# Causal mask carried in the unused contraction rows of q and k, in a fused attention and gated-convolution kernel

## The chip, the cores and the metric

The kernel runs on one core of a Trainium2 chip. The core has five engines with queues of their own: TensorE (PE, with its weight loads shown as PEld), VectorE (DVE), ScalarE (ACT), GpSimd (POOL) and SyncE (SP), which issues most of the DMAs. Each engine takes its instructions strictly in the order in which they were written; semaphores join the queues. The metric is the device time of one execution in microseconds.

## The reference

q, k and v are (8, 8, 576, 64) in float32, for 8 batches and 8 heads. f (8, 8, 576) holds forget gates. An attention with decay and a causal mask feeds a feed-forward layer whose gate is a convolution over the sequence:

```
scores = q @ k.T / sqrt(64) + cum[query] - cum[key]     # cum = cumsum(log(clip(f, 1e-4, 1)))
scores[key > query] = -1e9
attn = softmax(scores);  x = (attn @ v), heads side by side, (8, 576, 512)
h = relu(x @ w_in)                                        # (8, 576, 1024)
gate = sigmoid(conv of h over the sequence, 3 taps per channel)
out = (h * gate) @ w_out                                  # (8, 576, 512)
```

## The kernel before

**Half batches.** The attention is worked in 16 half batches (`hb`) of four heads. A sequence of 576 is cut into four key blocks of 128 and a tail of 64. Scores are computed with keys on the partitions. For each pair of heads there is one task for the four diagonal blocks (`sd`), two for the blocks below the diagonal (`so`), and for each half batch one for the tail (`st`). ScalarE takes the exponential of each (`ed`, `eo`, `et`), PE multiplies by v with a column of ones beside it (`pv`), VectorE divides (`n` the reciprocal, `m` the product), and the result is turned for the next layer by PE (`t`) and copied out (`tx`). The feed-forward tasks are, for each batch and each of 8 channel blocks: `f` on PE (w_in), `r` on ACT (relu), `c` and `d` on DVE (convolution), `a` on ACT, `g` on DVE (gate); then `o` on PE (w_out), `e` and `s` (copy out and store).

**Even and odd rows.** A float32 value is used as bf16 through its upper half. The turned q and k have 128 rows for 64 elements: the odd rows are the upper halves, the even rows are the lower halves, which are of no use. The contraction on PE runs over all 128 rows, so the even rows are free to carry something else. In the kernel before, three of them carry the decay and the rest are zero. For half batches 0 and 1, q and k are loaded plain and turned by PE (`tp`), then copied out by `turned_qk` (`cl`). The others are turned by a DMA (`load_qk`, task `q{hb}.{side}`, L180). In half batches 2 to 7 a clamp on VectorE (`cl{hb}.{side}`, L186) multiplies each row by 0 or 1 and adds the row's constant; then `rw{hb}` writes the decay rows by two small DMAs (L202, L203) from the DRAM tile `image`. In half batches 8 to 15 `fi{hb}` overwrites the even rows by DMAs from `blank` (zeros) and `image`. Half batch 0 adds the decay by two more matmuls per block (`by_matmul`).

**The causal mask** is applied in two ways. In half batches 0 to 7 (`MASK_PE`) PE first writes -1e30 above the diagonal into the bank with a matmul of `ident` and `mask` (L320) and adds the scores to it. In half batches 8 to 15 ScalarE writes the exponentials in float32 to `pd` or `p3`, and POOL copies them to `pp` or `pt` with an affine select that puts zeros above the diagonal (L356, L335; tasks `md`, `mt`).

**Order.** Nothing is scheduled while the program runs. The string `ORDER` is one list of task names; `Plan.play` goes through it and writes each task's instructions to its engines, and gives out buffers from rooms of fixed size (4 PSUM tiles `ps`, 6 of `pp`, 5 of `ht`, 4 of `u`). Where a task has several possible engines, `@` behind its name chooses one. The dependencies that the instructions wait for are those of the data and of the reused buffers.

## Time and profile before

| what | value |
|---|---|
| time, median of 3 runs | 247.56 us (247.29 to 249.18) |
| span of the profiled execution | 244.1 us |
| time of the profiled execution beside its span | not recorded; the median of the runs is 3.5 us above the span |
| granted TensorE clock | 0.999 |
| PE / DVE / ACT / POOL busy | 226.9 / 205.1 / 206.9 / 52.9 us |
| clamps, L186 | 12, 874 ns each, from 23.5 to 81.2 us |
| mask matmuls, L320 | 40, of which 32 are 128x512 |
| affine selects, L356 and L335 | 16 of 1244 ns, 8 of about 0.6 us |

A row of groups reads: line, engine, operation, out<-in with shapes, count | busy us, mean ns of one | idle time of the engine just before them and what ended it. A row of a timeline reads: start, duration, engine, line, operation, and in brackets the idle time before it with what ended it. A row of windows gives the stretch, its length, the busy time of each engine, the granted clock, the DMA share and the rate. In the chain, `issue` is time in which the engine waited for nothing that the profile shows; SPq, DVEq and so on are the engines' own issue work.

### The profile page before, as it was taken

How to read it: one execution, taken by the hardware profiler on the slowest of the kernel's cores; microseconds unless marked ns; L12 is line 12 of the kernel's file. 1: busy time of each engine (PE TensorE's matmuls, PEld its weight loads, DVE VectorE, ACT ScalarE, POOL GpSimd, SP SyncE). 2: the span in 40 equal slices, each digit the busy share in tenths (PEclk: the TensorE clock that was granted, in tenths of full speed). 3: DMA queues.
4: the chain of work that ended last, by engine and by line, in shares of the span. 5: the costliest groups of instructions: out<-in, count | busy, mean ns of one | idle time of the engine just before them, and what ended most of it. 6: DMA issues, size and time to landing. Idle time of an engine off the chain costs nothing.

```text
span 244.1 us, 6385 instructions
## 1 busy us (share of the span) xinstructions
PE 226.9 (93%) x2627; PEld 145.0 (59%) x2627; DVE 205.1 (84%) x323; ACT 206.9 (85%) x278; POOL 52.9 (22%) x77
## 2 busy tenths in 40 slices
...
GB/s 192 328 159 243 304 204 192 202 253 279 204 188 205 228 158 240 229 314 186 198 256 246 187 209 257 273 134 222 194 260 188 236 140 3 168 157 62 142 86 216
DMA packets 120176, 49.68 MB, mean 204 GB/s; under 512 B 109759, under 2 KB 110271, under 8 KB 120147
## 3 DMA queue, kind: packets, MB, share of 16 engines
...
q10 hardware_dynamic: 166, 0.31, 0.4%
...
HBM read 21.11 MB, written 10.17 MB: 128 GB/s over the span
## 4 chain that ended last, share of the span: by engine, by line
PE 78%; DVE 7%; DMA 6%; ACT 4%; issue 1%; ACTq 1%; SPq 1%; DVEq 0%
PE ps L474 24%; PE ps L429 20%; PE ps L312 15%; PE ps L389 7%; DMA qk<-in_q_dram 3%; PE ps L320 3%; PE ps L394 3%; PE ps L166 2%; PE ps L414 2%; DVE u L446 2%; ACT pp L370 2%; DMA pd<-in_moe_conv_w_dram 2%; DVE u L448 2%; DVE qk L186 1%; DMA qk<-image 1%
## 5 line engine op out<-in xcount | busy, mean ns | idle before, releaser
L429 PE MATMUL ps<-xt,w_in_f 128*128 128x512 f16 (+1 forms) x512 | 69.9, 286 | 0.0
L370 ACT ACTIVATE pp<-ps 128x1024 f16<-128x1024 f32 x64 | 64.7, 1032 | 4.2 <-PE ps L312 2.7
L474 PE MATMUL ps<-w_out_f,hg 128*128 128x512 f16 x288 | 66.8, 379 | 0.0
L312 PE MATMUL ps<-qk 128*128 128x128 bf16 (+2 forms) x576 | 63.4, 240 | 1.6 <-ACT pp L353 0.8
L446 DVE SCALAR_TENSOR_TENSOR u<-ht,cwt 128x576 f32<-128x576 f16 x64 | 52.7, 837 | 3.6 <-ACT ht L440 3.4
L451 ACT ACTIVATE hg<-u,cw 128x576 f16<-128x576 f32 x64 | 48.7, 782 | 5.9 <-DVE u L448 5.8
L448 DVE SCALAR_TENSOR_TENSOR u<-ht,cwt,u 128x576 f32<-128x576 f16 x64 | 53.2, 846 | 0.5
L429 PEld LDWEIGHTS <-w_in_f 128*128 128x128 f16 x512 | 34.3, 98 | 28.5
L312 PEld LDWEIGHTS <-qk 128*128 128x128 bf16 x576 | 39.2, 98 | 19.8 <-issue 3.3
L440 ACT ACTIVATE ht<-ps 128x576 f16<-128x576 f32 x64 | 41.0, 663 | 6.0 <-DVE hg L458 2.7
L474 PEld LDWEIGHTS <-hg 128*128 128x128 f16 x288 | 26.9, 98 | 28.8
L458 DVE SCALAR_TENSOR_TENSOR hg<-hg,ht 128x576 f16<-128x576 f16 x51 | 38.7, 771 | 0.6 <-ACT hg L451 0.5
L356 POOL TENSOR_SCALAR_AFFINE_SELECT pp<-pd 128x1024 f16<-128x1024 f32 x16 | 19.7, 1244 | 53.6 <-ACT pd L353 53.6
L389 PE MATMUL ps<-va,pp 128*128 128x65 f16 x640 | 24.8, 193 | 1.1 <-DVE va L217 1.0
L389 PEld LDWEIGHTS <-pp 128*128 128x128 f16 x640 | 22.6, 97 | 3.7 <-DVE va L217 1.3
L405 DVE TENSOR_TENSOR xm<-ps,rc 128x896 f16<-128x896 f32 (+1 forms) x32 | 23.9, 751 | 0.5
L353 ACT ACTIVATE pp<-ps 128x1024 f16<-128x1024 f32 x16 | 16.6, 1039 | 4.7 <-PE ps L312 3.9
L353 ACT ACTIVATE pd<-ps 128x1024 f32<-128x1024 f32 x16 | 16.2, 1023 | 1.2 <-PE ps L312 1.0
L217 POOL CAST va<-vf 128x1024 f16<-128x1024 f32 x8 | 10.0, 1252 | 32.1 <-DMA vf<-in_v_dram 27.8
L320 PE MATMUL ps<-mask,ident 128*128 128x512 bf16 (+1 forms) x40 | 14.3, 359 | 1.5 <-ACT pp L370 0.8
L403 DVE RECIPROCAL rc<-ps 128x14 f32<-128x14 f32 (+1 forms) x32 | 6.7, 208 | 8.6 <-PE ps L394 5.5
L479 ACT COPY ob<-ps 128x1024 f32<-128x1024 f32 (+1 forms) x14 | 12.9, 919 | 0.3 <-issue 0.2
...
## 6 DMA issues: line engine op xcount, KB each, us to landing
...
```

The source lines that it names most:

```text
L312: nc.tensor.matmul(o, tk[:, h * S + k0:h * S + k0 + 128], tq[:, h * S + q0:h * S + q0 + n], start=first, stop=last and not by_matmul(hb, h))
L353: nc.scalar.activation(o, ps_of(f"sd{i}").rearrange("p (s c) -> p s c", s=2), AF.Exp, scale=SCALE)
L370: nc.scalar.activation(pair(i)[:, s, 512:1536], ps_of(f"so{i}.{s}"), AF.Exp, scale=SCALE)
L389: nc.tensor.matmul(ps[:, c:c + D + 1], block(hb, h, m, n), va[:, h, m, 0:D + 1], start=(m == 0), stop=(m == n))
L405: nc.vector.tensor_tensor(xm[:, CUT * D * u:CUT * D * u + nj * k * D].rearrange("p (j x d) -> p j x d", x=k, d=D), got[:, :, :, 0:D], r.un ...
L429: nc.tensor.matmul(ps[:, t0:t1], w_in_f16[:, cc, 128 * ff:128 * (ff + 1)], xt[:, cc // 2, x:x + t1 - t0], start=(cc == 0), stop=(cc == NCC ...
L440: nc.scalar.activation(ht_of(b, ff)[:, 2:2 + S], ps_of(f"f{b}.{ff}")[:, 0:S], AF.Relu, scale=1.0 if (b, ff) in LATE else 0.5)
L446: nc.vector.scalar_tensor_tensor(u, ht[:, 1:1 + S], cwt[:, ff, 0:1], ht[:, 2:2 + S], op0=ALU.mult, op1=ALU.add)
L448: nc.vector.scalar_tensor_tensor(u, ht[:, 3:3 + S], cwt[:, ff, 1:2], u, op0=ALU.mult, op1=ALU.add)
L451: nc.scalar.activation(hg_of(b, ff), u_t[slot[f"c{b}.{ff}", "u"]], AF.Sigmoid if (b, ff) in LATE else AF.Tanh, scale=cw[:, ff, 1:2])
L458: nc.vector.scalar_tensor_tensor(hv, hv, 1.0, ht_of(b, ff)[:, 2:2 + S], op0=ALU.add, op1=ALU.mult)
L474: nc.tensor.matmul(ps[:, 512 * (c % 2):512 * (c % 2 + 1)], w, w_out_f16[:, ff, :], start=(ff == 0), stop=(ff == NFF - 1))
```

## The change

The mask moves into the contraction. 55 of the 60 free even rows get a pattern, the same for every head: each row stands for a group of 6 positions of a 128-block (22 groups for blocks 0 and 1, 22 for 2 and 3, 11 for the tail). In q's row the values are powers of two that fall by 2^21 from one position of the group to the next; in k's row they are negative powers of two that rise by 2^21 per position and stay at the top behind the group. The product is -2^11 or below where the key lies after the query, and tiny elsewhere, in the off-diagonal blocks too. So `masked` with its matmuls (L320) is gone, and so are the affine selects and the tiles `pd` and `p3`; the exponentials of all half batches are written straight to `pp` and `pt`. The tail's scores use 64 partitions, not 128.

The pattern gets into the even rows in three ways:
- Half batches 0 and 1: PE turns the odd halves alone, to partitions 0 to 63. The pattern is computed densely on VectorE for partitions 64 to 127 of one head (`dense`), and copied to the other heads and to half batch 1 (`px0` on VectorE, `px1` on POOL).
- Half batches 2 to 7: the clamp becomes `blend`, a SCALAR_TENSOR_TENSOR that multiplies each row by 0 or 1 and adds the pattern tile `edge`, read again for each of the four heads. `edge` is written by `spread` (task `pi`) on POOL.
- Half batches 8 to 15: the fill reads from `shape`, a DRAM copy of the even rows of `edge`, in place of `blank`; two DMAs per half batch as before.

Four rows carry the decay now (two for q, two for k), so `rw` writes 2 rows by each of its two DMAs, and `image` is written by 4 DMAs, not 3. The identities and selectors are built by POOL, not VectorE, and the memsets are gathered in `pads` (task `pd`). In `ORDER`, `px0.0 px0.1` stand ahead of `dcs`, `pd` ahead of `va0.0`, `px1.0 px1.1 pi` behind `va0.1`; all `md`, `mt` are taken out, each `fi` is a `rw` in the same place, and all else keeps its place. All twelve blends are given to VectorE. The core of the diff:

```diff
+    BLEND = (2, 3, 4, 5, 6, 7,)
...
-    NCL = 8
-    MASK_PE = (0, 1, 2, 3, 4, 5, 6, 7,)
-    NPD, NP3 = 2, 2
...
-            nc.tensor.transpose(o[:, 128 * j:128 * (j + 1)], i[:, 128 * j:128 * (j + 1)], ident_b)
+            nc.tensor.transpose(o[0:64, 128 * j:128 * (j + 1)], i[:, 128 * j + 1:128 * (j + 1):2], ident_b)
...
-    def clamp(hb, h0, nh, side):
-        t = (stq_t, stk_t)[side][hb % RING].bitcast(U16)[:, h0 * S:(h0 + nh) * S]
-        nc.vector.tensor_scalar(t, t, lim[:, 2 * side:2 * side + 1], lim[:, 2 * side + 1:2 * side + 2],
-                                op0=ALU.mult, op1=ALU.add)
...
+    def blend(hb, side, e):
+        t = (stq_t, stk_t)[side][hb % RING].bitcast(U16)[:, 0:HS].rearrange("p (h s) -> p h s", h=HH)
+        pattern = edge[:, side].bitcast(U16).unsqueeze(1).broadcast_to((128, HH, S))
+        if e == "DVE":
+            nc.vector.scalar_tensor_tensor(t, t, lit[:, 2:3], pattern, op0=ALU.mult, op1=ALU.add)
+        else:
+            nc.gpsimd.tensor_scalar(t, t, lit[:, 2:3], None, op0=ALU.mult)
+            nc.gpsimd.tensor_tensor(t, t, pattern, op=ALU.add)
...
+    def edge_rows(t, side, e):
+        copy = {"ACT": nc.scalar.copy, "POOL": nc.gpsimd.tensor_copy, "DVE": nc.vector.tensor_copy}[e]
+        h = 1 if t == 0 else 0
+        o = qk_t[t][64:128, HS * side + h * S:HS * (side + 1)].rearrange("p (h s) -> p h s", s=S)
+        copy(o, qk_t[0][64:128, HS * side:HS * side + S].unsqueeze(1).broadcast_to((64, HH - h, S)))
...
     def fill(hb):
-        nc.sync.dma_start(even_rows(hb, 4, 60, 0, 2 * HS).rearrange("p (h s) -> p h s", s=2 * S),
-                          blank.unsqueeze(1).broadcast_to((60, HH, 2 * S)))
-        nc.sync.dma_start(even_rows(hb, 0, 4, 0, 2 * HS).rearrange("j (a x) -> j a x", a=2),
+        t = qk_t[hb % RING]
+        nc.sync.dma_start(rows(t, 8, 2, 60, 0, 2 * HS).rearrange("p (a h s) -> p a h s", a=2, s=2 * S),
+                          shape.rearrange("p a h s -> p a (h s)").unsqueeze(2).broadcast_to((60, 2, 2, 2 * S)))
+        nc.sync.dma_start(rows(t, 0, 2, 4, 0, 2 * HS).rearrange("j (a x) -> j a x", a=2),
...
-        nc.sync.dma_start(even_rows(hb, 1, 2, HS + h0 * S, 2 * HS), image[1:3, 1, c, :].rearrange("j h s -> j (h s)"))
+        c, t = slice(hb * HH, (hb + 1) * HH), qk_t[hb % RING]
+        for side in range(2):
+            r = 2 * side
+            nc.sync.dma_start(rows(t, 64 + r if hb < NPL else 2 * r, 1 if hb < NPL else 2, 2, HS * side, HS * (side + 1)),
+                              image[r:r + 2, side, c, :].rearrange("j h s -> j (h s)"))
...
+    turns = xm_t[0].bitcast(FP32), xm_t[1].bitcast(FP32), u_t[2], u_t[3], xt_t[0].rearrange("p a x -> p (a x)").bitcast(FP32)[:, 0:S]
+    base = turns[3]
+    dense = [qk_t[0][64:128, HS * side:HS * side + S].bitcast(U16) for side in range(2)]
+    SPAN, WHOLE, BOTH = GROUP + (FAR + 0.003) / STEP, float(-128 * STEP), float(128 * (FIRST - STEP + 2 * 127) + 32768)
...
+    def count(p0, per):
+        i = turns[0][p0:128].bitcast(I32)
+        nc.gpsimd.iota(i[:, 0:512], pattern=[[22 * GROUP, 2], [0, 2], [1, 128]], base=4 * GROUP, channel_multiplier=-per)
+        nc.gpsimd.iota(i[:, 512:S], pattern=[[1, SL]], base=48 * GROUP, channel_multiplier=-per)
+        return i
...
+    i = count(64, GROUP)
+    nc.gpsimd.memset(base, float(128 * (127 + TOP)))
+    nc.gpsimd.memset(base[:, 0:512].rearrange("p (a j s) -> p a j s", a=2, j=2)[:, :, 1], float(128 * (127 + LOW)))
...
-    nc.vector.tensor_scalar(mask, hfx, lit[:, 0:1], -1e30, op0=ALU.is_lt, op1=ALU.mult)
...
+    at, w, x = (turns[j][64:128] for j in range(3))
+    nc.vector.tensor_scalar(w, i, SPAN, None, op0=ALU.min)
+    nc.vector.scalar_tensor_tensor(x, w, WHOLE, base[64:128], op0=ALU.mult, op1=ALU.add)
+    nc.vector.scalar_tensor_tensor(at, w, 0.0, x, op0=ALU.is_ge, op1=ALU.mult)
+    nc.vector.scalar_tensor_tensor(dense[0], w, GROUP - 0.5, at, op0=ALU.is_le, op1=ALU.mult)
+    nc.vector.tensor_scalar(x, x, -1.0, BOTH, op0=ALU.mult, op1=ALU.add)
+    nc.vector.scalar_tensor_tensor(dense[1], w, 1.0, x, op0=ALU.is_ge, op1=ALU.mult)
+    for side, n, value in ((0, 4, 1.0), (0, 2, 0.0), (1, 4, 0.0), (1, 2, -1.0)):
+        nc.vector.memset(dense[side][0:n].bitcast(BF16), value)
...
+    nc.gpsimd.tensor_scalar(ident_b, hfx, lit[:, 0:1], None, op0=ALU.is_equal)
...
+    nc.gpsimd.tensor_scalar(ident, hfx, lit[:, 0:1], None, op0=ALU.is_equal)
...
+    def spread():
+        p = lit[:, 0:1]
+        nc.gpsimd.tensor_scalar(lit[:, 3:4], p, 7.5, None, op0=ALU.is_ge)
+        nc.gpsimd.tensor_scalar(lit[:, 4:5], lit[:, 2:3], 0.0, lit[:, 3:4], op0=ALU.is_equal, op1=ALU.mult)
...
+        at, w, x, y = (turns[j] for j in (0, 1, 2, 4))
+        i = count(0, GROUP // 2)
+        nc.gpsimd.tensor_scalar(w, i, SPAN, None, op0=ALU.min)
+        nc.gpsimd.tensor_scalar(x, w, WHOLE, None, op0=ALU.mult)
+        nc.gpsimd.tensor_tensor(x, x, base, op=ALU.add)
+        for side in range(2):
+            nc.gpsimd.tensor_scalar(at, w, float(side), None, op0=ALU.is_ge)
+            if side == 0:
+                nc.gpsimd.tensor_scalar(y, w, GROUP - 0.5, None, op0=ALU.is_le)
+                nc.gpsimd.tensor_tensor(at, at, y, op=ALU.mult)
+            else:
+                nc.gpsimd.tensor_scalar(x, x, -1.0, BOTH, op0=ALU.mult, op1=ALU.add)
+            nc.gpsimd.tensor_tensor(at, at, x, op=ALU.mult)
+            nc.gpsimd.tensor_scalar(edge[:, side].bitcast(U16), at, lit[:, 4:5], lit[:, 6 + side:7 + side], op0=ALU.mult, op1=ALU.add)
...
+    def pads():
+        for t in range(NVA):
+            nc.gpsimd.memset(va_t[t][:, :, :, D:VW], 1.0)
+            nc.gpsimd.memset(va_t[t][64:128, :, NKB - 1, 0:D], 0.0)
...
+        for t in range(NPT):
+            nc.gpsimd.memset(pt_t[t][64:128], 0.0)
...
-        nc.sync.dma_start(blank, zero[0:60])
...
+        even = bass.AP(tensor=edge.tensor, offset=int(edge.offset) + 8 * 2 * S, ap=[[2 * 2 * S, 60], [S, 2], [1, S]])
+        for h in range(2):
+            nc.sync.dma_start(shape[:, :, h], even)
...
+    def scores(o, hb, h, k0, q0, n, m=128):
...
-    def masked(o, n, j):
-        nc.tensor.matmul(o, ident, mask[:, 0:j].unsqueeze(1).broadcast_to((128, n, j)), start=True, stop=False)
...
     def tail_scores(hb):
-        on = hb in MASK_PE
-        if on:
-            masked(ps_of(f"st{hb}")[:, 0:HH * SL], HH, SL)
...
-            if on:
-                masked(ps[:, 512 * s:512 * (s + 1)], 4, 128)
...
-    def diag_mask(i):
-        nc.gpsimd.affine_select(pair(i)[:, :, 0:512].rearrange("p s (m j) -> p s m j", j=128),
-                                pd_t[slot[f"ed{i}", "pd"]].rearrange("p s (m j) -> p s m j", j=128),
-                                pattern=[[0, 2], [0, 4], [1, 128]], base=0, channel_multiplier=-1,
-                                compare_op=ALU.is_ge, fill=0.0)
...
+    add("ki", "SP", ["dck"], decay_image)
+    add("zc", "SP", ["pi", "pd"], constants)
...
+    add("pi", "POOL", [], spread)
+    add("pd", "POOL", [], pads)
+    for t in range(NPL):
+        for side in range(2):
+            add(f"px{t}.{side}", "POOL/DVE/ACT", [], lambda e, t=t, side=side: edge_rows(t, side, e))
...
-                add(f"rw{hb}", "SP", [f"cl{hb}.{p}.{side}" for p, side in parts] + ["ki"], lambda hb=hb: rows_of(hb))
-                ready = [[f"rw{hb}"]] * 2
+                add(f"rw{hb}", "SP", ["ki"] + px, lambda hb=hb: rows_of(hb))
+                ready = [[f"rw{hb}"] + [f"cl{hb}.{p}.{side}" for side in range(2)] for p in range(2)]
...
-            if hb < NCL:
-                for side in range(2):
-                    add(f"cl{hb}.{side}", "DVE", [f"q{hb}.{side}"], lambda hb=hb, side=side: clamp(hb, 0, 4, side))
-                add(f"rw{hb}", "SP", [f"cl{hb}.{side}" for side in range(2)] + ["ki"], lambda hb=hb: rows_of(hb))
-                ready = [[f"rw{hb}"]] * 2
+                add(f"q{hb}.{side}", "SP", old, lambda hb=hb, side=side: load_qk(hb, side))
+                if hb in BLEND:
+                    add(f"cl{hb}.{side}", "POOL/DVE", [f"q{hb}.{side}", "pi"], lambda e, hb=hb, side=side: blend(hb, side, e))
+            if hb in BLEND:
+                add(f"rw{hb}", "SP", ["ki"] + [f"cl{hb}.{side}" for side in range(2)], lambda hb=hb: rows_of(hb))
             else:
-                add(f"fi{hb}", "SP", [f"q{hb}.0", f"q{hb}.1", "zc", "ki"], lambda hb=hb: fill(hb))
-                ready = [[f"fi{hb}"]] * 2
+                add(f"rw{hb}", "SP", ["ki", "zc"] + [f"q{hb}.{side}" for side in range(2)], lambda hb=hb: fill(hb))
+            ready = [[f"rw{hb}"]] * 2
...
-            if hb not in MASK_PE:
-                add(f"md{i}", "POOL", [f"ed{i}"], lambda i=i: diag_mask(i), give=[("pd", f"ed{i}")])
+            add(f"ed{i}", "ACT", [f"sd{i}"], lambda i=i: diag_exp(i), give=[("ps", f"sd{i}")])
```

Three places show what the change does to the queues. First POOL, behind the start-up memsets. Before, the second cast of half batch 0's v (L219) is followed by a cast of w_in:

```order
L263 MEMSET va_94 64x4x64
L217 CAST va_91<-vf_89 128x4x4x64
L219 CAST va_91<-vf_89 64x4x64
L518 CAST w_in_f_69<-ob_125 128x2x512
L217 CAST va_92<-vf_89 128x4x4x64
L518 CAST w_in_f_69<-ob_126 128x2x512
```

Now (L221, L223 are those casts) the copies `px1` and then all of `spread` stand between; its last rows and the cast of w_in (L537) are the second piece:

```order
L221 CAST va_90<-vf_88 128x4x4x64
L223 CAST va_90<-vf_88 64x4x64
L189 COPY qk_85<-qk_84 64x2304 x2
L272 TENSOR_SCALAR lit<-lit 128x1
L273 TENSOR_SCALAR lit<-lit 128x1
```

```order
L292 TENSOR_TENSOR xm_104<-xm_104,u_118 128x576
L293 TENSOR_SCALAR edge<-xm_104,lit 128x576
L286 TENSOR_SCALAR xm_104<-xm_105 128x576
L291 TENSOR_SCALAR u_118<-u_118 128x576
L292 TENSOR_TENSOR xm_104<-xm_104,u_118 128x576
L293 TENSOR_SCALAR edge<-xm_104,lit 128x576
L537 CAST w_in_f_69<-ob_121 128x2x512
```

Between the two pieces stand the rest of the eight small operations, an iota and six operations on 128x576.

Second, VectorE at half batch 2, whose q and k lie in one tile (`qk_87` before, `qk_86` now). Before, the clamps wait for a DMA alone, and the norms of half batch 0 (L403, L405) follow:

```order
L174 TENSOR_SCALAR qk_86<-ps_131,lim 128x1152 [waits PE_49,Activation_49]
L186 TENSOR_SCALAR qk_87<-qk_87,lim 128x2304 [waits DMAHW2_49]
L186 TENSOR_SCALAR qk_87<-qk_87,lim 128x2304 [waits DMAHW6_49]
L403 RECIPROCAL rc_110<-ps_130 128x14 [waits PE_49,Activation_49]
L405 TENSOR_TENSOR xm_108<-ps_130,rc_110 128x896 [waits DVE_49]
```

Now each blend (L180) waits for POOL too, with the same norms (L422, L424) behind it:

```order
L168 COPY qk_85<-ps_127 64x1152 [waits PE_49,Activation_49]
L180 SCALAR_TENSOR_TENSOR qk_86<-qk_86,lit,edge 128x2304 [waits DMAHW3_49,Pool_49]
L180 SCALAR_TENSOR_TENSOR qk_86<-qk_86,lit,edge 128x2304 [waits DMAHW6_49,Pool_49]
L422 RECIPROCAL rc_106<-ps_126 128x14 [waits PE_49,Activation_49]
L424 TENSOR_TENSOR xm_104<-ps_126,rc_106 128x896 [waits DVE_49]
```

The place in the queue is the same; the operation and the wait are new.

Third, SP behind the loads of w_in. Before, the decay rows of half batch 2 (task `rw2`, to `qk_87`) stand ahead of the turned loads of half batches 3 and 4:

```order
L510 DMA ob_128<-in_moe_w_in_dram 128x2x512
L202 DMA qk_87<-image 1x2304
L203 DMA qk_87<-image 2x2304
L180 DMA_TRANSPOSE qk_88<-in_q_dram 128x2304
L180 DMA_TRANSPOSE qk_88<-in_k_dram 128x2304
L180 DMA_TRANSPOSE qk_85<-in_k_dram 128x2304
```

Now (L206 and L172, half batch 2 in `qk_86`) they stand there as well, and wait for the blends:

```order
L529 DMA ob_124<-in_moe_w_in_dram 128x2x512
L206 DMA qk_86<-image 2x2304 x2
L172 DMA_TRANSPOSE qk_87<-in_q_dram 128x2304
L172 DMA_TRANSPOSE qk_87<-in_k_dram 128x2304
L172 DMA_TRANSPOSE qk_84<-in_k_dram 128x2304
```

Nothing is reordered here; the rows behind `rw2` follow it as before.

164 lines of the change are left out of this document (60 added, 104 removed).

## The prediction

> **What bounds the kernel now.** I read the page first: the busy times, then the chain that ended last, by line.
>
> ```profile
> span 244.1 us, 6385 instructions
> ...
> PE 226.9 (93%) x2627; PEld 145.0 (59%) x2627; DVE 205.1 (84%) x323; ACT 206.9 (85%) x278; POOL 52.9 (22%) x77
> ...
> by line: PE ps L474 24.2%; PE ps L429 20.3%; PE ps L312 14.6%; PE ps L389 6.8%; DMA qk<-in_q_dram 3.0%; PE ps L320 2.7%; PE ps L394 2.5%; PE ps L166 2.4%; PE ps L414 2.2%; DVE u L446 2.1%; ACT pp L370 2.1%; DMA pd<-in_moe_conv_w_dram 2.0%;
> ```
>
> PE's lines carry most of the chain (the masks, L320, 2.7% of it), but 93, 84 and 85% are averages over stages, so the next view is the busy time by stage (the columns stand in its first row; times from the span's start).
>
> ```profile
> core 0: us, PE busy (x) PEld busy (x) DVE busy (x) ACT busy (x) POOL busy (x), PEclk, DMA share, GB/s
> 25.20:36.50 11.30, 10.12 (x173) 7.83 (x173) 4.46 (x9) 8.34 (x10) 5.14 (x5) 1.00 1.19 253
> 36.50:60.10 23.60, 20.27 (x278) 13.56 (x275) 23.26 (x35) 21.76 (x31) 4.39 (x4) 1.00 1.08 231
> 60.10:89.10 29.00, 29.00 (x338) 18.55 (x337) 27.24 (x42) 27.25 (x38) 5.42 (x5) 1.00 1.07 208
> 89.10:230.00 140.90, 140.79 (x1582) 86.00 (x1580) 131.57 (x197) 128.86 (x180) 31.24 (x31) 1.00 0.90 196
> ```
>
> Four stages with three limits. From 25 to 36 VectorE works 4.5 us out of 11. From 36.5 to 60 VectorE has 0.3 us to spare in 23.6 and PE has 3.3. From 60 to 89 PE has no gap, and VectorE only 1.8 us. After 89 PE is full for 141 us with VectorE 9 us under it. The chain in order of time says the same:
>
> ```profile
> 36.53 0.76 DVE xt L417
> 37.29 1.45 DVE qk L186 x2
> ...
> 57.77 1.01 DVE xm L405
> 58.82 0.83 PE ps L414 x9
> ...
> 222.65 3.92 PE ps L429 x32
> ```
>
> Between 36.5 and 58.8 the end hangs on VectorE and the loads behind its clamps, and the clamp itself (L186) is on the chain. From 58.8 on it hangs on PE, bar a few pieces. The change takes work off PE and puts it on VectorE, in just the stages where VectorE is full or nearly so.
>
> **What a blend costs.** Twelve clamps (half batches 2 to 7, q and k) turn from a TENSOR_SCALAR on one tensor into a SCALAR_TENSOR_TENSOR on two. Groups by line:
>
> ```profile
> L186 DVE TENSOR_SCALAR qk<-qk,lim 128x2304 uint16<-128x2304 uint16 x12 | 10.3, 874 | 2.3 <-DMA qk<-in_q_dram 2.3
> L458 DVE SCALAR_TENSOR_TENSOR hg<-hg,ht 128x576 f16<-128x576 f16 x51 | 38.7, 771 | 0.6 <-ACT hg L451 0.5
> L456 DVE TENSOR_TENSOR hg<-hg,ht 128x576 f16<-128x576 f16 x13 | 5.5, 451 | 1.0 <-ACT hg L451 1.0
> L405 DVE TENSOR_TENSOR xm<-ps,rc 128x256 f16<-128x256 f32 x16 | 6.6, 415 | 0.2
> L405 DVE TENSOR_TENSOR xm<-ps,rc 128x896 f16<-128x896 f32 x16 | 17.4, 1087 | 0.3
> ```
>
> The two forms of L405 give a slope of (1087 - 415) / 640 = 1.05 ns per element for an operation with two inputs at full width. Over 2304 elements that is 415 + 2048 x 1.05 = 2.57 us. The nearest row by operation is L458, all 16 bits wide and still 771 ns for 576 elements, on that same slope; so I take 2.55 us, **1.68 us more than a clamp**. The lower end is L456, a TENSOR_TENSOR on the same 16-bit tensors in 451 ns: 451 + 1728 x 0.525 = 1.36 us, 0.48 more. The upper end is four times L458, 3.08 us, 2.2 more.
>
> The Trainium skill, "VectorE: DVE Perf Modes", section "What auto-detection actually checks", says that two elements go through per cycle when every tensor is 16 bits wide with step 1. By that rule the blend would take the lower end; L458 meets its condition and does not show it, L456 does. What it would give is the second rival below.
>
> **Step A, the pattern comes late.** The blends of half batch 2 need the pattern that `spread` writes on POOL. On POOL it stands behind the casts va0 and two copies `px1` of 64x2304 each. POOL's rows:
>
> ```profile
> 16.53 1.04 POOL L217 CAST va<-vf 128x1024 f16<-128x1024 f32 x1 [10.07 <-DMA vf<-in_v_dram]
> 17.51 0.39 POOL L219 CAST va<-vf 64x256 f16<-64x256 f32 x1
> 25.70 1.04 POOL L518 CAST w_in_f<-ob 128x1024 f16<-128x1024 f32 x1 [7.80 <-DMA ob<-in_moe_w_in_dram]
> ...
> L356 POOL TENSOR_SCALAR_AFFINE_SELECT pp<-pd 128x1024 f16<-128x1024 f32 x16 | 19.7, 1244 | 53.6 <-ACT pd L353 53.6
> L335 POOL TENSOR_SCALAR_AFFINE_SELECT pt<-p 128x256 f16<-128x256 f32 x4 | 2.3, 584 | 4.1 <-ACT p L332 4.1
> L255 POOL MEMSET zero<- 64x1152 bf16 x1 | 1.0, 1049 | 0.0
> L262 POOL MEMSET va<- 128x40 f16 x4 | 0.5, 133 | 0.2
> L228 POOL IOTA hix<- 128x128 int32 x1 | 0.2, 234 | 0.0
> ```
>
> The casts wait for the load of v, so POOL is at 17.9 us there whatever the new memsets ahead cost (it idled 10 us). Then: two copies at the cast's rate (1.04 us for 1024), 2.3 us each, to 22.5. Eight operations of 128x1 at 0.133, 1.1 us. An iota of 576, at most 4.5 x 0.234 = 1.0. Twelve operations on 128x576, of which four have two inputs. For these the page has no row; between L335 and L356 the cost at 576 elements is 584 + 320 x 0.86 = 0.86 us, and I take that for all: 10.3 us. POOL ends `spread` at **35.0 us**, with q's half of the pattern ready four operations earlier, at 31.6. The lower end (the cast's 0.58 us per operation, the memset's rate for the copies, half the iota) is 30.7. The upper end (two-input operations twice as long, copies at L356's rate) is 39.4.
>
> The Trainium skill, "GPSIMD Engine Reference", section 3.1, gives 4497 ns for a two-input operation on 2048 elements; as an estimate that is 1.27 us for 576, and `spread` would end at 36.6 instead. No run so far shows such an operation.
>
> VectorE and PE around that time, with the load that follows a clamp:
>
> ```profile
> 23.50 1.67 DVE L186 TENSOR_SCALAR qk<-qk,lim 128x2304 uint16<-128x2304 uint16 x2 [2.25 <-DMA qk<-in_q_dram]
> ...
> 25.37 0.58 SPq L203 DMA_DIRECT2D qk<-image  x1
> ...
> 22.71 3.01 DMA qk<-image
> ...
> 31.16 0.39 PE L320 MATMUL ps<-mask,ident 128*128 128x512 bf16 x1
> ...
> 34.94 0.39 PE L320 MATMUL ps<-mask,ident 128*128 128x512 bf16 x1
> 35.16 0.39 PE L312 MATMUL ps<-qk 128*128 128x128 bf16 x4
> ```
>
> Before, the two clamps ended at 25.17, `rw2` was issued at 25.37 and, at the 3.01 us of its neighbour, landed at 28.4; PE came to `sd5`, the first scores of half batch 2, at 31.16. Now the first blend runs from 31.6 to 34.2, the second from 35.0 to 37.5. `rw2` lands near 41, and `sd5` follows its mask-free start there: before, its first score came 0.22 us behind the mask, at 31.38. PE is **9.6 us late**; the 2.8 us that `rw2` used to be early are spent. Everything is queued behind this. On VectorE the norms `n0.0` to `m1.1` stand behind the blends, on SP the loads of q and k for half batches 3 and 4 stand behind `rw2`, and on PE all that follows stands behind `sd5`. Three more masks are gone between there and 36.5, at 0.22 us each (the step from 34.94 to 35.16), so **+9.0 us** at 36.5.
>
> What else is added at the start is covered by this wait. VectorE gets six operations on 64x576, at 0.76 us each by the row below, and two copies `px0` that at the clamp's rate take under 0.9 each:
>
> ```profile
> 9.83 0.76 DVE L274 SCALAR_TENSOR_TENSOR kc<-u,kc 64x576 bf16<-64x576 f32 x1
> ```
>
> That is some 6 us, against the selectors and the mask that it built before and now leaves to POOL; `dck` and the first scores come perhaps 1.5 us later. `px1` ends at 22.5, and the load that waits for it, `rw1`, went at 22.71 anyway. All that is over before 31 us and would cost up to 1.5 us only if the wait at the blends were gone.
>
> **Steps B and C, ten blends.** The six of half batches 3 to 5 run from the pair on the chain at 37.29 to 59.23, the four of 6 and 7 from 75.36 on, the last two at 80.40:
>
> ```profile
> 59.23 0.87 DVE L186 TENSOR_SCALAR qk<-qk,lim 128x2304 uint16<-128x2304 uint16 x1
> ...
> 75.36 0.87 DVE L186 TENSOR_SCALAR qk<-qk,lim 128x2304 uint16<-128x2304 uint16 x1
> ...
> 80.40 1.66 DVE L186 TENSOR_SCALAR qk<-qk,lim 128x2304 uint16<-128x2304 uint16 x2
> ```
>
> B: from 36.5 to 60 VectorE has 0.3 us to spare: 6 x 1.68 = 10.1, **+10 us**. PE's masks here hide nothing, since PE already waits.
>
> C: 4 x 1.68 = 6.7 us against 1.8 us of slack from 60 to 89: **+4.9 us**. PE meets VectorE again here:
>
> ```profile
> 88.35 0.76 DVE L417 COPY xt<-ps 128x1152 f16<-128x1152 f16 x1 [0.18 <-PE ps L414]
> ...
> 89.56 1.14 PE L429 MATMUL ps<-xt,w_in_f 128*128 128x512 f16 x8
> ```
>
> The matmuls of batch 2 start 0.45 us behind the copy that feeds them, so PE takes the delay over nearly whole.
>
> **Step D, after 89.** PE is full and stays so. Of the masks, those left there, by the same windows for L320 alone:
>
> ```profile
> 60.10:89.10 29.00, 4.13 (x12) 1.17 (x12) 1.00 1.07 208
> 89.10:230.00 140.90, 2.06 (x6) 0.49 (x5) 1.00 0.90 196
> ```
>
> Six at 0.22 or less: **-1.0 us**. The others stand in stages where VectorE, not PE, sets the time, and are worth nothing beyond what A counted. The POOL selects of half batches 8 to 15 go away, 19.7 us and some, but POOL is 22% busy and PE never idles for them; the fills move the same bytes from `shape` as from `blank`.
>
> **Sum:** 9.0 + 10.1 + 4.9 - 1.0 = +23.0 us on the profiled span of 244.1, so about 267. The profiled execution has no time of its own beside the span; the median of the runs is 247.56, 3.5 above it. I carry the 3.5 over: 247.56 + 23.0 = 270.6, and say **271**.
>
> **The rivals.**
> 1. *The pattern is slower or quicker than 35.0.* Slower: at 39.4 the second blend ends at 42.0, +4.5, 275; POOL and VectorE working at once, or blends at the upper end, take it to 281. Quicker: at 30.7 the second blend waits for the first and ends at 33.5, -4.0, 267. Nothing in the profile decides, as no POOL arithmetic of this kind is there.
> 2. *The blend goes at two elements per cycle* (1.36 us). A loses 1.2, to +7.8; B is 6 x 0.48 = 2.9; C is 1.9 against a slack of 1.8, 0.1, so PE sets the pace there again and gains its 12 masks from 60 to 89, 2.3 us at 0.22 for the wide and half that for the narrow ones. 7.8 + 2.9 + 0.1 - 2.3 - 1.0 = +7.5, 255. L456 speaks for it, L458 against.
> 3. *Faster: the masks come off PE's path and nothing replaces them.* The chain gives L320 2.7%, 6.6 us: 241. It needs the pattern by 23.5 us, when the q load lands, and a blend dearer than a clamp by no more than 6.6 / 12 = 0.55 us. POOL is free at 17.9, the copies take 4.2 or more, and 1.4 us would be left for work that the rows put at 12.5.
> 4. *VectorE's order holds slack that I don't see*, so that PE takes over only part of B and C (half, 7 us less): 263. The gap of 0.45 us at 89 speaks against it.
>
> **How the numbers follow.** The forecast, with its own spread of 265 to 277: 0.62. Slower than that, up to 281 and beyond: 0.14. Rival 4, 258 to 265: 0.09. Rival 2, near 255: 0.09. Rival 3, 241: 0.04. No change: 0.02, it would need a loss of the size of the gain. The range that holds the time 8 times in 10 is 257 to 280. 1% is about what a measurement of this kernel tells from no change. Faster by over 1%: 0.04; within 1%: 0.02; slower by over 1%: 0.94.
>
> **What would show it.** The first blend starts near 32 us and waits for POOL, not for its load. The twelve blends take 2.5 to 2.6 us each. PE idles some 10 us before the first scores of half batch 2. VectorE is full from there to the copies that feed batch 2, and those matmuls start some 24 us later than at 89.56. From there to the end the length is the old 154.5 us less 1. A blend below 1.5 us makes B and C wrong; a first blend that waits for its load makes A wrong; a later part that also grows shows a cost that I have not seen.

## The result and the profile after

The changed kernel takes 285.68 us (median; 284.89 to 287.03), the kernel before on the same chip 248.37: a ratio of 1.152, with a 95% interval of 1.146 to 1.159. The ratio leaves out one run of the kernel before, 251.86 us, 1.8% above its fastest. The forecast was 271, its range 257 to 280. The sign was right, and the three places were right; the size was 15 us short.

The page of the changed kernel, the span, the busy times and the chain by engine:

```profile
span 283.1 us, 6314 instructions
...
PE 233.0 (82%) x2587; PEld 148.6 (53%) x2587; DVE 230.8 (82%) x321; ACT 206.5 (73%) x278; POOL 64.0 (23%) x85
...
PE 59%; DVE 16%; POOL 9%; DMA 6%; issue 4%; ACT 3%; SPq 0%; ACTq 0%; POOLq 0%; DVEq 0%
```

PE works 6 us more, in a span that is 39 us longer, so its share fell from 93 to 82%. POOL, busy for only 23% of the span, holds 9% of the chain, some 25 us: an engine that the averages show as idle sets the time for part of the way.

The 39 us are laid out by three copies on VectorE that end the stretches of the prediction: the last copy of batch 0 (36.53 before), the last of batch 1 and the first of batch 2. Before:

```profile
60.02 0.75 DVE L417 COPY xt<-ps 128x1152 f16<-128x1152 f16 x1
...
87.42 0.76 DVE L417 COPY xt<-ps 128x1152 f16<-128x1152 f16 x1
```

After:

```profile
55.52 0.76 DVE L436 COPY xt<-ps 128x1152 f16<-128x1152 f16 x1 [0.38 <-PE ps L433]
...
91.39 0.75 DVE L436 COPY xt<-ps 128x1152 f16<-128x1152 f16 x1
...
124.82 0.76 DVE L436 COPY xt<-ps 128x1152 f16<-128x1152 f16 x1 [0.37 <-PE ps L433]
```

| stretch | before | after | measured | predicted |
|---|---|---|---|---|
| A, to the last copy of batch 0 | 36.5 | 55.5 | +19.0 | +9.0 |
| B, to the last copy of batch 1 | 23.5 | 35.9 | +12.4 | +10.1 |
| C, to the first copy of batch 2 | 27.4 | 33.4 | +6.0 | +4.9 |
| D, to the end | 156.6 | 158.3 | +1.7 | -1.0 |

By the medians the change costs 37.3 us and by these spans 39.0. In every execution on record with both, the time is 1.7 to 1.8 us above the span. By that the profiled execution of the kernel before took some 245.9 us, an estimate; it was quicker than every run of that kernel on record (246.4 us or more), and the 3.5 us that the forecast carried over were 1.8 for the changed kernel. So a difference against the row of before, here and below, is some 2 us or more larger than that of the medians, and which stretch of that execution was quicker than usual is not known.

Stretch A is where the forecast is 10 us short. POOL's own queue there, with `spread` from L272 to L293:

```profile
17.67 4.16 POOL L189 COPY qk<-qk 64x2304 bf16<-64x2304 bf16 x2
21.92 0.23 POOL L272 TENSOR_SCALAR lit<-lit 128x1 f32<-128x1 f32 x1
...
25.34 1.67 POOL L282 TENSOR_SCALAR xm<-xm 128x576 f32<-128x576 int32 x1
27.09 1.66 POOL L283 TENSOR_SCALAR u<-xm 128x576 f32<-128x576 f32 x1
28.84 1.40 POOL L284 TENSOR_TENSOR u<-u,u 128x576 f32<-128x576 f32 x1
...
36.64 0.82 POOL L293 TENSOR_SCALAR edge<-xm,lit 128x576 uint16<-128x576 f32 x1
...
42.74 0.82 POOL L293 TENSOR_SCALAR edge<-xm,lit 128x576 uint16<-128x576 f32 x1
```

The copies start at 17.67, as forecast (17.9), and take 4.2 us where 4.6 were forecast. The twelve wide operations run from 25.34 to 43.56, 18.2 us instead of 10.3. And it is not the two-input ones that are dear: the TENSOR_TENSORs take 1.40 each, the TENSOR_SCALARs 1.65 to 1.89, and only the last operation of each side takes 0.82.

The twelve blends by their line, with the shortest, the median and the longest in ns:

```profile
L180 DVE SCALAR_TENSOR_TENSOR qk<-qk,lit,edge x12: 2536/2608/3360, 37.5 to 116.1; 128x2304 uint16<-128x2304 uint16 x12
```

VectorE and PE around the two that wait for the pattern, in order of time:

```profile
37.50 3.12 DVE L180 SCALAR_TENSOR_TENSOR qk<-qk,lit,edge 128x2304 uint16<-128x2304 uint16 x1 [11.76 <-POOL edge L293]
...
43.60 3.36 DVE L180 SCALAR_TENSOR_TENSOR qk<-qk,lit,edge 128x2304 uint16<-128x2304 uint16 x1 [2.98 <-POOL edge L293]
46.89 0.23 DVE L422 RECIPROCAL rc<-ps 128x14 f32<-128x14 f32 x1
47.15 1.09 DVE L424 TENSOR_TENSOR xm<-ps,rc 128x896 f16<-128x896 f32 x1
...
48.30 0.60 PE L408 MATMUL ps<-va,pp 128*128 128x65 f16 x8 [14.95 <-DVE xm L424]
...
49.52 1.04 PE L354 MATMUL ps<-qk 128*128 128x128 bf16 x8
```

The blend's median of 2.61 us is the 2.55 of the prediction; the two that run beside POOL are stretched to 3.1 and 3.4. PE stands still for 15 us, and what it waits for at 48.30 is not `rw2`'s load but the norm L424, queued on VectorE behind the second blend: the values of half batch 0 (`m0.0`) have to leave their bank of PSUM before PE may go on to `pv0.1` and `sd5`.

### The profile page after: what moved, and what is told of

Read it like the earlier page. It is cut to its first block, busy times and chain, and to the rows that moved or that the text cites. A ratio compares the mean times of both kernels' runs of the same rounds, so it can differ in the third digit from the quotient of the medians.

```text
span 283.1 us, 6314 instructions
## 1 busy us (share of the span) xinstructions
PE 233.0 (82%) x2587; PEld 148.6 (53%) x2587; DVE 230.8 (82%) x321; ACT 206.5 (73%) x278; POOL 64.0 (23%) x85
## 4 chain that ended last, share of the span: by engine, by line
PE 59%; DVE 16%; POOL 9%; DMA 6%; issue 4%; ACT 3%; SPq 0%; ACTq 0%; POOLq 0%; DVEq 0%
PE ps L493 20%; PE ps L448 18%; PE ps L354 11%; DVE qk L180 8%; PE ps L408 6%; DMA vf<-in_v_dram 3%; DVE xm L424 3%; PE ps L413 2%; DVE hg L477 2%; DMA u<-in_f_dram 2%; PE ps L433 2%; DMA qk<-in_k_dram 2%; POOL qk L189 1%; DVE u L467 1%; DVE u L465 1%
## 5 line engine op out<-in xcount | busy, mean ns | idle before, releaser
L354 PE MATMUL ps<-qk 128*128 128x128 bf16 (+3 forms) x576 | 66.0, 249 | 14.6 <-DVE xm L424 8.6
L448 PE MATMUL ps<-xt,w_in_f 128*128 128x512 f16 (+1 forms) x512 | 72.0, 291 | 1.3 <-DVE xt L436 1.1
L389 ACT ACTIVATE pp<-ps 128x1024 f16<-128x1024 f32 x64 | 64.3, 1026 | 11.3 <-PE ps L354 8.5
L354 PEld LDWEIGHTS <-qk 128*128 128x128 bf16 (+1 forms) x576 | 39.0, 103 | 32.5 <-issue 18.4
L448 PEld LDWEIGHTS <-w_in_f 128*128 128x128 f16 x512 | 35.1, 99 | 31.0 <-issue 2.9
L459 ACT ACTIVATE ht<-ps 128x576 f16<-128x576 f32 x64 | 40.5, 656 | 14.8 <-DVE hg L477 8.5
L379 ACT ACTIVATE pp<-ps 128x1024 f16<-128x1024 f32 x32 | 32.6, 1024 | 22.2 <-PE ps L354 19.7
L180 DVE SCALAR_TENSOR_TENSOR qk<-qk,lit,edge 128x2304 uint16<-128x2304 uint16 x12 | 32.8, 2744 | 14.7 <-POOL edge L293 14.7
L408 PE MATMUL ps<-va,pp 128*128 128x65 f16 x640 | 27.3, 200 | 17.6 <-DVE xm L424 15.5
L408 PEld LDWEIGHTS <-pp 128*128 128x128 f16 x640 | 24.9, 102 | 20.8 <-issue 16.4
L221 POOL CAST va<-vf 128x1024 f16<-128x1024 f32 x8 | 12.5, 1580 | 64.0 <-ACT pp L389 24.9
L424 DVE TENSOR_TENSOR xm<-ps,rc 128x896 f16<-128x896 f32 (+1 forms) x32 | 23.9, 750 | 0.5
L223 POOL CAST va<-vf 64x256 f16<-64x256 f32 x6 | 4.0, 670 | 83.6 <-ACT pp L389 38.1
L422 DVE RECIPROCAL rc<-ps 128x14 f32<-128x14 f32 (+1 forms) x32 | 6.6, 208 | 7.7 <-PE ps L408 5.0
L537 POOL CAST w_out_f<-ob 128x1024 f16<-128x1024 f32 x4 | 7.1, 1765 | 22.3 <-DMA ob<-in_moe_w_out_dram 22.3
```

The source lines that it names most:

```text
L180: nc.vector.scalar_tensor_tensor(t, t, lit[:, 2:3], pattern, op0=ALU.mult, op1=ALU.add)
L354: nc.tensor.matmul(o, tk[:, h * S + k0:h * S + k0 + m], tq[:, h * S + q0:h * S + q0 + n], start=True, stop=not by_matmul(hb, h))
L379: nc.scalar.activation(pair(i)[:, :, 0:512], ps_of(f"sd{i}").rearrange("p (s c) -> p s c", s=2), AF.Exp, scale=SCALE)
L389: nc.scalar.activation(pair(i)[:, s, 512:1536], ps_of(f"so{i}.{s}"), AF.Exp, scale=SCALE)
L408: nc.tensor.matmul(ps[:, c:c + D + 1], block(hb, h, m, n), va[:, h, m, 0:D + 1], start=(m == 0), stop=(m == n))
L448: nc.tensor.matmul(ps[:, t0:t1], w_in_f16[:, cc, 128 * ff:128 * (ff + 1)], xt[:, cc // 2, x:x + t1 - t0], start=(cc == 0), stop=(cc == NCC ...
```

## The experiments

All times are medians beside runs of the kernel before on the same chip (247.8 to 249.6). The same stretches for all of them, from the same three copies, so that each edit can be read where it acts (us):

| kernel | A | B | C | D | span | median |
|---|---|---|---|---|---|---|
| before | 36.5 | 23.5 | 27.4 | 156.6 | 244.1 | 247.6 |
| the change | 55.5 | 35.9 | 33.4 | 158.3 | 283.1 | 285.7 |
| pattern on VectorE | 46.0 | 35.1 | 33.4 | 158.7 | 273.3 | 274.8 |
| clamp's price, no wait | 40.5 | 24.6 | 26.5 | 158.4 | 249.9 | 251.7 |
| dear blends, no wait | 39.7 | 35.6 | 33.4 | 157.6 | 266.2 | 268.0 |
| wait, clamp's price | 55.3 | 22.7 | 28.7 | 158.7 | 265.3 | 267.2 |
| numbers from columns | 56.2 | 36.5 | 33.4 | 158.5 | 284.6 | 286.4 |
| two blended, four more filled* | 45.5 | 30.6 | 34.1 | 158.8 | 269.0 | 272.5 |
| blend in two steps | 55.1 | 32.6 | 32.1 | 158.4 | 278.2 | 279.5 |
| two columns each | 58.1 | 36.1 | 33.0 | 158.7 | 285.9 | 287.4 |
| light start | 37.7 | 24.4 | 26.7 | 159.0 | 247.7 | 250.1 |
| VectorE and two steps | 44.8 | 33.4 | 32.1 | 158.9 | 269.2 | 271.2 |
| PE fed, 62 matmuls | 55.2 | 35.6 | 33.4 | 159.2 | 283.4 | 284.8 |
| PE fed, 70 matmuls | 54.0 | 35.9 | 33.4 | 161.3 | 284.6 | 286.2 |

*Of half batches 2 to 7: 2 and 3 blended, 4 to 7 filled.

The theory tested was that three terms add: the wait for POOL's pattern, the dearer blends up to the last copy of batch 1, and those up to batch 2. The rivals: the wait's cost is not POOL's, or the wait and what comes behind it are one effect.

**The pattern on VectorE.**

```diff
-        nc.gpsimd.tensor_scalar(x, w, WHOLE, None, op0=ALU.mult)
-        nc.gpsimd.tensor_tensor(x, x, base, op=ALU.add)
+        nc.vector.scalar_tensor_tensor(x, w, WHOLE, base, op0=ALU.mult, op1=ALU.add)
...
- px1.1@POOL pi q2.1
+ px1.1@POOL q2.1
...
- cl0.1.1@DVE wi1
+ cl0.1.1@DVE pi wi1
```

> The pattern is written by VectorE, ahead of the blends and behind the copies of half batch 0, in 13 operations (VectorE takes two steps in one where POOL needs two operations); nothing else is changed. Theory (the wait for POOL's pattern, the ten dearer blends from half batch 3 to 5 and those of 6 and 7 add up: 19.0, 12.4 and 6.0 us in the trace of the change): VectorE has the pattern near 29 us instead of 43.6, the two blends end near 34 and their load lands near 37, so that the copy that ends this part comes about 5 us later than before instead of 19. Time: 285.7 - 13.6 = 272 us. Rival (POOL's pattern is not what PE waits for; the load behind the blends or the lower clock is): 283 to 286 us, and PE still idles some 15 us there.

274.8 us, 1.108 times before (1.102 to 1.114): 10.9 less than the change, where 13.6 were expected. On the spans it is 9.8 less, 9.5 out of A and 0.8 out of B. VectorE's rows:

```profile
22.28 0.46 DVE L282 TENSOR_SCALAR xm<-xm 128x576 f32<-128x576 int32 x1 [2.80 <-POOL xm L239]
...
26.93 0.58 DVE L291 TENSOR_SCALAR edge<-xm,lit 128x576 uint16<-128x576 f32 x1
27.43 1.34 DVE L168 COPY qk<-ps 64x1152 bf16<-64x1152 bf16 x1
```

The wide operations of the same pattern take VectorE 5.2 us, against 18.2 on POOL. Two things eat up part of the gain: VectorE first waits 2.8 us for POOL's count, and the copies of half batch 1 (L168) now stand behind the pattern, where PE waits for one of them (us, times, longest):

```profile
PE ps L352 <- DVE qk L168: 5.0, 1, 5.0
```

**The clamp's price and no wait; dear blends and no wait.** In both, the pattern is one memset in place of all that `spread` did, ahead of the casts; the last two lines of the diff are in the first alone:

```diff
     def spread():
...
+        nc.gpsimd.memset(edge, 0.0)
...
-        nc.gpsimd.memset(plus, 1.0)
-        nc.gpsimd.memset(minus, -1.0)
+        nc.gpsimd.memset(plus, 0.0)
+        nc.gpsimd.memset(minus, 0.0)
...
-            nc.vector.scalar_tensor_tensor(t, t, lit[:, 2:3], pattern, op0=ALU.mult, op1=ALU.add)
+            nc.vector.tensor_scalar(t, t, lit[:, 2:3], lit[:, 2:3], op0=ALU.mult, op1=ALU.add)
```

> The pattern is one memset of zeros early on POOL, and the twelve blends are one-tensor operations as in the kernel before (the clamp's form and price). Left out: pattern, mask and decay in half batches 2 to 15. PE has no masks. Theory (the wait and the dearer blends are all that costs): 242 to 248 us, as PE loses its masks and nothing takes their place, with the copy at the end of the first part back near 36.5 us. Rival (the rest of the change, its fills, copies, loads and the part after 89 us, costs by itself): 252 us or more.

> The pattern is one memset of zeros early on POOL, so that no blend waits for it; the twelve blends keep their two-tensor form and price. Left out: pattern, mask and decay in half batches 2 to 15. Theory (the terms are independent and add): no wait for the pattern, so 285.7 - 19.0 + about 1 for the two dearer blends of half batch 2 = 268 us, with the blends 2.5 to 2.6 us each and VectorE full from 36 to about 100 us. Rival (the wait at half batch 2 also slows what comes behind it, by PE's lower clock or by the order, so that the later blends cost less without it): 255 to 262 us.

**The wait and the clamp's price.** The same one-tensor operation for half batches 3 to 7 only; pattern and `spread` as in the change.

```diff
-            nc.vector.scalar_tensor_tensor(t, t, lit[:, 2:3], pattern, op0=ALU.mult, op1=ALU.add)
+            if hb == 2:
+                nc.vector.scalar_tensor_tensor(t, t, lit[:, 2:3], pattern, op0=ALU.mult, op1=ALU.add)
+            else:
+                nc.vector.tensor_scalar(t, t, lit[:, 2:3], lit[:, 2:3], op0=ALU.mult, op1=ALU.add)
```

> The pattern comes from POOL as in the change, and half batch 2 is blended with it; the ten blends of half batches 3 to 7 are one-tensor operations at the clamp's price. Left out: mask and decay in half batches 3 to 7. Theory (the terms add): the wait of 19.0 us stays, 12.4 and 6.0 us go: 285.7 - 18.4 = 267 us, 1 to 3 less if PE then gains the masks that it no longer has. Rival (behind the wait VectorE is no longer what sets the time, so that dearer blends cost little): 278 us or more.

The three measured 251.7, 268.0 and 267.2 us; 1.016 (1.011 to 1.021), 1.082 (1.077 to 1.086) and 1.080 (1.073 to 1.086) times before. Counted from the first, the wait (with the two dear blends of half batch 2) costs 15.5 by itself, the dear blends without a wait 16.4, together 31.9; both at once cost 34.0 (285.7 - 251.7). So the terms add but for 2 us, and 268 and 267 are the expected figures. The table shows where: without the wait B and C stay at 35.6 and 33.4; without the dear blends they go back to 22.7 and 28.7 with the wait left at 55.3. The rival that they are one effect is out.

The first of the three did not come in as expected. With a blend at the clamp's price, with nothing to wait for and no mask on PE, the kernel is still 3.9 us slower than before by the medians, where 242 to 248 were expected. On the spans it is 5.8: A +3.9, B +1.1, C -0.9, D +1.7. For A, two rows of VectorE's start, and behind them what PE waits for up to the copies of batch 2 (us in all, times, longest):

```profile
13.42 1.53 DVE L295 TENSOR_SCALAR kc<-u 128x576 bf16<-128x576 f32 x1
14.98 0.76 DVE L296 SCALAR_TENSOR_TENSOR kc<-u,kc 64x576 bf16<-64x576 f32 x1
```

```profile
PE ps L163 <- ACT qk L168: 2.1, 1, 2.1
...
PE ps L335 <- DVE kc L296: 1.4, 1, 1.4
```

The decay rows `kc` end at 15.7 where they ended at 10.6 before, behind the pattern of half batch 0 and its copies: 5.1 us later, where the prediction had said 1.5.

**A light start**, on top of the clamp's price and no wait: the pattern of half batch 0 as zeros, the selectors back on VectorE.

```diff
-    nc.vector.scalar_tensor_tensor(x, w, WHOLE, base[64:128], op0=ALU.mult, op1=ALU.add)
...
+    for side in range(2):
+        nc.vector.memset(dense[side].bitcast(BF16), 0.0)
...
-    nc.gpsimd.tensor_scalar(ident_b, hfx, lit[:, 0:1], None, op0=ALU.is_equal)
+    nc.vector.tensor_scalar(ident_b, hfx, lit[:, 0:1], None, op0=ALU.is_equal)
```

> As the run with the clamp's price and no wait (251.7 us), but the start has almost none of the change's work: the six operations and four memsets that make the pattern of half batch 0 on VectorE are two memsets of zeros, the count and the base for them on POOL are gone, and the five selectors are on VectorE again, as in the kernel before. Left out: pattern, mask and decay in all half batches. If the 3.9 us that the run with the clamp's price is over the kernel before lie in the start (its copy at the end of the first part comes at 40.5 instead of 36.5), that copy comes at 36 to 37 us and the time is 247 to 249. If they lie elsewhere, it stays at 251 to 252.

250.1 us (1.011, 1.004 to 1.018), above the expected 247 to 249; A is 37.7. So 2.8 of the 3.9 us that the start lost are had back. Of the 3.6 us by which the span is still above that of before, 2.4 stand in D.

**What makes POOL's operations slow.** First, the numbers from columns of a tile instead of from the instruction:

```diff
-        nc.gpsimd.tensor_scalar(x, w, WHOLE, None, op0=ALU.mult)
+        nc.gpsimd.tensor_scalar(x, w, imm[:, 1:2], None, op0=ALU.mult)
```

> The seven operations of the pattern on POOL that take one tensor and numbers written into the instruction (1.65 to 1.89 us each in the trace of the change) take the same numbers from columns of a tile instead, as the two operations do that write the pattern and took 0.82 us. Nothing is left out. If the written-in number is what makes them slow, they fall to about 0.8, the pattern ends near 37.7 us instead of 43.6, and the time falls by 5 to 7 us, to 279 to 281. If it is the 32-bit result or something else that the fast two don't share, the durations stay at 1.65 and the time at 285 to 287.

(There are six such operations, not seven.) 286.4 us, no gain. One group did change:

```profile
L289 POOL TENSOR_SCALAR xm<-xm,imm 128x576 f32<-128x576 f32 x2 | 5.9, 2942 | 0.1
...
L286 POOL TENSOR_SCALAR u<-xm,imm 128x576 f32<-128x576 f32 x1 | 1.7, 1732 | 0.1
...
L294 POOL TENSOR_SCALAR u<-u,imm 128x576 f32<-128x576 f32 x1 | 0.8, 816 | 0.0
```

L294, the only one with two steps, fell from 1.89 to 0.82 us; the product with one step (L286) stayed at 1.73. So neither the written-in number alone nor the 32-bit result is what makes an operation slow. Then two steps with two columns for all six (the diff is against the run above):

```diff
-        nc.gpsimd.tensor_scalar(x, w, imm[:, 1:2], None, op0=ALU.mult)
+        nc.gpsimd.tensor_scalar(x, w, imm[:, 1:2], imm[:, 2:3], op0=ALU.mult, op1=ALU.add)
-        nc.gpsimd.tensor_scalar(w, i, imm[:, 0:1], None, op0=ALU.min)
+        nc.gpsimd.tensor_scalar(w, i, imm[:, 0:1], imm[:, 3:4], op0=ALU.min, op1=ALU.mult)
```

> As the run with numbers taken from columns (286.4 us), but each of the six one-tensor operations of the pattern on POOL also gets a second step that changes nothing (times one, or plus zero), its number from a column too. In that run the one operation with two columns had gone from 1.89 to 0.82 us, and those with one step had stayed at 1.73. Nothing is left out. If the two-step form with two columns is what makes an operation fast, whatever the steps are, five more operations go from 1.73 to 0.82, the pattern ends 4.5 us earlier than there and the time is 280 to 282. If it is the pair of a multiplication and an addition that is fast, only the product with WHOLE gets faster (0.9 us) and the time is 284 to 286.

287.4 us. The second theory holds for the operations and misses the time:

```profile
L285 POOL TENSOR_SCALAR xm<-xm,imm 128x576 f32<-128x576 int32 x1 | 2.3, 2318 | 0.1
L291 POOL TENSOR_SCALAR xt<-xm,imm 128x576 f32<-128x576 f32 x1 | 2.3, 2297 | 0.0
...
L286 POOL TENSOR_SCALAR u<-xm,imm 128x576 f32<-128x576 f32 x1 | 0.8, 826 | 0.1
L294 POOL TENSOR_SCALAR u<-u,imm 128x576 f32<-128x576 f32 x1 | 0.8, 824 | 0.0
```

A product and a sum from two columns take 0.82 us; a minimum or a comparison with a product takes 2.3, dearer than alone (1.73). Four of the six steps are a minimum or a comparison, so POOL loses more on them than it gains.

**The blend in two steps.**

```diff
-            nc.vector.scalar_tensor_tensor(t, t, lit[:, 2:3], pattern, op0=ALU.mult, op1=ALU.add)
+            nc.vector.tensor_scalar(t, t, lit[:, 2:3], None, op0=ALU.mult)
+            nc.vector.tensor_tensor(t, t, pattern, op=ALU.add)
```

> Each blend is two operations, the one-tensor multiplication of the clamp's form (0.87 us) and a TENSOR_TENSOR that adds the pattern, instead of one SCALAR_TENSOR_TENSOR of 2.6 us. Nothing is left out. If a TENSOR_TENSOR on 16-bit tensors goes at the rate of the gate's (451 ns for 576, 1.36 us for 2304), a blend is 2.2 us and ten blends in full stages are 3.5 to 4 us cheaper: 281 to 283 us. If it goes at the rate of the SCALAR_TENSOR_TENSOR, a blend is 3.4 us: 292 to 295 us.

279.5 us (1.128, 1.124 to 1.132), 6.2 less than the change, where 3.5 to 4 were expected. On the spans it is 4.9 less; B is 3.3 shorter and C 1.3. The addition by itself, with the shortest, the median and the longest:

```profile
L181 DVE TENSOR_TENSOR qk<-qk,edge x12: 1357/1358/2164, 38.3 to 112.3; 128x2304 uint16<-128x2304 uint16 x12
```

1.36 us is what L456's 451 ns for 576 elements gave. Two operations on the same tensors are quicker than the one that does both: 0.85 + 1.36 = 2.21 against 2.61.

**Two half batches blended, four filled**, with the pattern on VectorE:

```diff
-    BLEND = (2, 3, 4, 5, 6, 7,)
+    BLEND = (2, 3,)
...
- rw3 f0.3
+ rw3 zc f0.3
```

> The pattern on VectorE as in the run that moved it there (274.8 us), and only half batches 2 and 3 are blended; 4 to 7 get their even rows by transfers, as 8 to 15 do, so eight blends leave VectorE and four transfers of 540 KB and four of 36 KB are added, most of them between 45 and 100 us. Nothing is left out. Theory (VectorE's dearer blends set the time there): 8 x 2.6 = 20.8 us leave VectorE, which has some 18 us too much there against the kernel before; PE takes over as the bound, near 256 us (274.8 - 18.4 and a little back as the two of half batch 3 stay). Rival (the DMA queues are full there: a share of 1.07 to 1.08 in the kernel before): 2.3 MB more at some 230 GB/s are 10 us, 266 us or more.

272.5 us (1.103, 1.095 to 1.111). The rival had it: VectorE has its time back, but between 46 and 116 us PE now waits 13.5 us, most of them for the fills,

```profile
PE ps L352 <- DMA qk<-shape: 8.1, 3, 3.3
```

and C, with no blend left in it, is as long as with four.

**Both gains,** the pattern on VectorE and the blend in two steps, by the two diffs above.

> The pattern on VectorE (274.8 us by itself) and each blend in two operations (279.5 by itself, 6.2 less than the change). Nothing is left out. If the two gains lie in different terms, the wait and the full stages, they add: 268 to 270 us, still 20 above the kernel before. If VectorE's stages were no longer full without the wait, less is gained: 272 to 275 us.

271.2 us (1.096, 1.090 to 1.101): of 10.9 and 6.2 us, 14.5 are had together, 2.6 less than the sum and between the two expectations. It is the fastest complete form of the change that was run, and 9.6% over the kernel before.

**PE's clock behind the wait.** In the change the granted clock (the third column from the right) falls after PE's last matmul, which ends at 33.3, and stays at half for the first 4.7 us of work:

```profile
35.00:36.00 1.00, 0.00 (x0) 0.00 (x0) 0.00 (x0) 0.42 (x1) 0.92 (x2) 1.00 0.00 0
36.00:37.00 1.00, 0.00 (x0) 0.00 (x0) 0.00 (x0) 0.00 (x0) 0.89 (x2) 0.51 0.00 0
...
52.00:53.00 1.00, 1.00 (x11) 0.65 (x9) 0.55 (x2) 0.00 (x0) 0.00 (x0) 0.50 1.25 219
53.00:54.00 1.00, 1.00 (x27) 0.94 (x24) 1.00 (x2) 0.80 (x1) 0.00 (x0) 0.95 1.16 255
```

Two runs fed PE, in `off_scores`, matmuls that nobody reads during the wait, the second with 70 instead of 62:

```diff
+        if (i, s) == (3, 0):
+            for _ in range(62):
+                nc.tensor.matmul(ps[:, 0:512], ident_b, stq_t[0][:, 0:512], start=True, stop=True)
```

> The change, and PE is given 62 matmuls of 512 columns that nobody reads, some 13 us, in the 15 us in which it waits for the blends of half batch 2; its scores before and after are the same, and nothing is left out. In the trace of the change the granted clock falls to 0.50 at 36.0, 2.7 us after PE's last matmul, and is back at 1.00 at 53, 4.7 us after PE has work again. If PE's idleness is what lowers the clock and PE's pace is what counts just behind the wait, the clock stays at 1.00 and the copy that ends the first part comes some 2 us before 55.5; the time is 283 to 284. If the clock is lowered by something else, or what follows takes the 2 us back (VectorE is full from there on), the time stays at 285 to 286.

> As the run in which PE was given 62 matmuls that nobody reads (284.8 us), but 70 of them, so that PE stops only about 0.2 us before its next work at 48.3 instead of 1.9. There the clock still fell to 0.50, from 49.7 to 53, some 3.4 us after PE had stopped at 46.3. If such a pause, even a short one, is what brings the fall, the clock now stays at 1.00 past 53, the copy that ends the first part comes at 53 to 54 instead of 55.2 to 55.5, and the time is 283 to 284.5. If the clock falls again with hardly a pause, something else lowers it.

With 62, PE paused for 1.9 us (46.4 to 48.3), and the clock fell all the same, at 49.6, 3.2 us after the pause had begun; with 70 it did not fall. The windows of the one and of the other:

```profile
48.00:49.00 1.00, 0.71 (x28) 0.65 (x27) 0.24 (x1) 0.36 (x1) 1.00 (x2) 1.00 0.07 18
...
50.00:53.00 3.00, 3.00 (x42) 2.64 (x40) 1.14 (x2) 1.41 (x2) 0.80 (x1) 0.50 1.27 156
```

```profile
50.00:52.00 2.00, 2.00 (x45) 1.70 (x41) 0.97 (x2) 1.97 (x3) 0.51 (x1) 1.00 1.43 84
52.00:54.00 2.00, 1.82 (x43) 1.52 (x41) 1.59 (x5) 1.28 (x2) 0.00 (x0) 1.00 1.14 257
```

So PE's pause is what lowered the clock here, and at full clock the copy comes at 54.0 instead of 55.5; 0.3 us of that is a pattern that was ready earlier, 1.2 the clock. The whole time does not show it: 284.8 (1.144, 1.134 to 1.155) and 286.2 us (1.151, 1.143 to 1.159) against 285.7, intervals that overlap. In the second profile PE also waited once, 2.3 us, for a load of `image` late in D, which the change's profile does not have.

## Why the prediction was wrong, and where it was right

**The step that failed is the price of POOL's wide operations in step A:** "between L335 and L356 the cost at 576 elements is 584 + 320 x 0.86 = 0.86 us, and I take that for all: 10.3 us". They took 18.2. The bounds failed with it: the upper one doubled only the two-input operations and ended `spread` at 39.4, while the dear ones were the minima and comparisons on one tensor, 1.65 us, and the end was 43.6. The eight operations of 128x1 took 2.6 instead of 1.1 us, the copies and the count 0.8 less than taken, an earlier start of 0.2 included. Together `spread` was 8.6 us later than 35.0. The other 1.4 of the 10 us missing in A: the second blend, stretched beside POOL, 3.36 instead of 2.55 (+0.8); PE at `sd5` 2.6 us behind that blend instead of 3.5, as a norm and not the load ended the wait (-0.9); and from there 6.0 us instead of 4.5 to the last copy (+1.5), of which the run with PE fed puts 1.2 on the lowered clock. The rows that were used are selects and casts, and they say nothing of a minimum on POOL. Bounds drawn from a select and a cast do not bound arithmetic, and the range was built as if they did.

The Trainium skill, "GPSIMD Engine Reference", section 3.1, gives the 4497 ns for a two-input operation of 2048 elements from which the prediction estimated 1.27 us for 576. The trace shows 1.40, a tenth above the estimate. That section has no measured time for a minimum or a comparison on one tensor, which cost most here.

**B, +12.4 for +10.1.** The mechanism is right: VectorE full, ten blends at 2.61. Six times 1.73 over the clamp are 10.4; the table gives 11.0 between the two runs without the wait (35.6 - 24.6), and 1.1 more that the run at the clamp's price shows without any dear blend (with the wait in it that run's B is 22.7, 0.8 less than before). What that 1.1 is stays open; it is less than the 2 us by which the profiled execution of the kernel before was quicker than its median.

**C, +6.0 for +4.9.** The term of the sum that failed is the slack of 1.8 us taken off 6.7. Between the two runs without the wait, C differs by 6.9 us (33.4 - 26.5), four times 1.73. So these four are paid in full, and no slack took any of it. Set against before it is 6.0 and not 6.9, since without the dear blends C is 0.9 shorter than before; with the wait in it, it is 1.3 longer, so that much depends on what comes ahead.

**D, +1.7 for -1.0**, and between +1.0 and +2.6 in every run but the one with the extra wait; so it belongs neither to the wait nor to the blends. The six masks are gone and PE's clock is full there, but PE's weight loads for the scores now show gaps,

```profile
  issue: 2.1, 9
```

nine in all, in the view of line L354 from 126.5 us on, and none in the same view of the kernel before. The step of the prediction that failed is a term that it put at nothing: the tail's scores, which the change narrows to 64 partitions of output, so that their weights have 64 columns and not 128. In the rows by shape these 40 loads (four heads in ten half batches) hold 1.8 us of idle time of the weight queue:

```profile
L354 PEld LDWEIGHTS <-qk 128*64 128x64 bf16 x40 | 2.0, 110 | 1.8 <-issue 1.5
```

The matmuls of the shape, in the kernel before (tails among the 76) and now:

```profile
L312 PE MATMUL ps<-qk 128*128 128x64 bf16 x76 | 9.4, 193 | 0.0
```

```profile
L354 PE MATMUL ps<-qk 128*128 128x64 bf16 x36 | 7.0, 194 | 0.2 <-DVE xm L424 0.2
L354 PE MATMUL ps<-qk 128*64 128x64 bf16 x40 | 3.1, 201 | 0.0
```

By the start times in the trace, PE's step into such a group of four and its step out of it are each some 0.1 us longer than the usual step of the same matmul. Over ten tails that is 1.9 us, where the six masks had taken 1.1; the other 0.9 is spread over other steps. The run at the clamp's price has the same 1.8 us at its tails. No run kept the tail at 128 columns, so the price is read from the traces and not tested by itself.

**The cover at the start.** "would cost up to 1.5 us only if the wait at the blends were gone": with the wait gone stretch A was 3.9 longer, and 2.8 of it went with a light start.

**The rivals.** The first (a slower pattern) named the mechanism, and its price stopped at 281. The second (two elements per cycle) is refuted for this operation, 2.61 us and not 1.36. The Trainium skill, "VectorE: DVE Perf Modes", section "What auto-detection actually checks", asks for 16-bit tensors with step 1 and also for a mode that is enabled for the operation; the prediction used the first condition alone. On the same tensors the TENSOR_TENSOR shows that rate (1.36) and the SCALAR_TENSOR_TENSOR does not (2.61). The third (faster, 241) is answered by the run at the clamp's price: even when a blend costs no more than a clamp and waits for nothing, the kernel is at 251.7, so the masks' share of the chain was not had with this start and this D. The fourth (slack in VectorE's order) is out, B and C came in full.
